# Where the weight steps of a two-layer Fourier and MLP kernel stand among its matrix products: fixed places in inner products instead of every second place

## Chip, cores and metric

One core of a Trainium2 chip runs the kernel alone. The metric is the device time in microseconds of one execution; 2741.95 us is the median of three runs (2740.89 to 2742.17). The engines are TensorE (PE, matrix products; PEld is its weight load), VectorE (DVE), ScalarE (ACT), GpSimd (POOL) and SyncE (SP), which here only issues DMAs. Each engine works through its own instructions in program order and waits for the others by semaphores.

## Reference

Two layers, each a Fourier mixing block and an MLP on 2048 tokens of width 576, with an inner width of 4608, in float32:

```python
def _A_ref(x, dft_seq_re, dft_seq_im, dft_hid_re, dft_hid_im):
    a = jnp.einsum("bsd,ed->bse", x, dft_hid_re)
    b = jnp.einsum("bsd,ed->bse", x, dft_hid_im)
    return jnp.einsum("ts,bse->bte", dft_seq_re, a) - jnp.einsum("ts,bse->bte", dft_seq_im, b)

def _B_ref(x, w1, b1, w2, b2):
    y = _layernorm(x, axis=-1)
    h = _gelu(jnp.einsum("bsd,df->bsf", y, w1) + b1)
    return jnp.einsum("bsf,fd->bsd", h, w2) + b2

x = x + _A_ref(_layernorm(x), ...)
x = x + _B_ref(_layernorm(x), ...)
x = x + _A_ref(_layernorm(x), ...)
x = x + _B_ref(_layernorm(x), ...)
```

Both layers use the same weights and the same Fourier matrices.

## The kernel before

**Arithmetic.** Every float32 factor is split into a high part in the type float32r and the low rest: ACT writes the high part (`hi`, `high`), VectorE subtracts it from the source (`lo`, `low`). A product is then three matmuls (high by high, high by low, low by high). On top of that, products of two-by-two blocks are done as seven block products instead of eight, numbered 1 to 7 and done in the order 1, 6, 2, 5, 7, 3, 4 (`ORDER`); the sums of blocks that this needs are made on VectorE and POOL ahead of it, and the products are put together while they are taken out of PSUM.

**Stages.** A layer runs the sequence transform (`Sequence`: the normalized input times the Fourier matrix along tokens; sixteen token tiles, the first two in plain products, fourteen by seven products each, `run`, L687 on), then for each half of the tokens the hidden transform (`hidden`, matrices from `dh`) and the MLP (`mlp`). All matmuls but the transposes are recorded at one line, L206, all adds at L196 and all subtracts at L199, since helpers issue them.

**The MLP of a half.** 18 inner products (`inner`, first weights w1, bias and gelu) and 9 times seven outer products (`outer`, second weights w2, two half-products each). A group is: an even inner product (7 block products of 7 matmuls of 512 columns), the four outer products of the first list in `OUTER` for the group before (1, 6, 5, 3: 8 half-products of 12 matmuls of 288 columns), an odd inner product, and the three outer products of the second list (7, 4, 2: 6 half-products); 49 + 96 + 49 + 72 = 266 matmuls. Behind each block product or half-product `advance()` is called. It counts the place within the group in `at[0]`: 0 to 6 are the even inner product, 7 to 14 the four outer products, 15 to 21 the odd inner product, 22 to 27 the three outer products; `at[1]` counts on without a reset. After `advance` of an outer half-product VectorE adds the bank to the sum in SBUF (L196, 128x576), which frees the bank; there are two pairs of banks for each side, so a bank is written again two half-products later, and the next inner product uses the same banks. In the slots of outer products and in the block products of the next inner one, `work` takes one of eight `step(n)`s that split gelu's results into parts.

**First weights' steps.** `weights()` (L272 on) is a generator that makes the 126 parts of the first weights (18 times seven) in layer 0: `load` brings four raw blocks of an inner product (`in_w`, four times 192 KB), `high(n)` and `low(n)` split part n (ACT L272, L273; VectorE L199, 128x384), POOL makes the next sum of blocks, and `keep(n)` stores the part to `w_parts` from ACT's queue and loads raw blocks for the next inner product on SP's queue. It yields after each `low(n)` with `high(n+1)`, and after each `keep(n)`: two pumps for a part. `pump()` takes it one yield on. In the sequence transform of layer 0 `pump()` is called twice behind each product but the third (product 2); in the MLP `advance` calls it; `load_w`, which loads parts for coming inner products from SP's queue, calls it as often as the part asked for is not yet made. Both halves and layer 1 read the parts back.

**Second weights' parts.** In the MLP of the first half of layer 0 the second weights are split too: `make(g)` gives fourteen steps for group g, a `hi` (ACT L1080) and a `lo` (VectorE L199, 128x576, and in most a subtract on POOL) for each of the seven parts, with the places at which `advance` takes them; parts needed by the first outer products are made one group ahead. `soon` puts stores and raw loads two places later.

**Queues.** SP issues nearly all loads and stores of activations, in program order, and a DMA that has to wait (for its target to be read out) holds up all behind it. `b1t` holds the first biases; it is loaded behind the sequence transform of layer 0.

Of the kernel before, what the change touches and what calls it, by code (L numbers as in the profile page):

```python
# [20 lines left out]
NG = NQ // 2  # L21
# [36 lines left out]
EXTRA_AT = 7424  # L58
EARLY_X = (12800, 9344, 8192)
EARLY_T = 10496  # L60
H_AT = (8704, 22400)
C2_AT = (OWN_AT, 37760)
Y_AT = (RN - Y_N, 0)
# [92 lines left out]
def spectral_mixer(ctx: ExitStack, tc: tile.TileContext, x, dh, c0, cs, w1, b1, w2, b2, out):  # L156
# [29 lines left out]
    b1t = const.tile([P, 2 * NQ], F32, name="b1t")  # L186
    middle = const.tile([P, 1], F32, name="middle")

    def dma(dst, src):
        nc.sync.dma_start(dst, src)  # L190
# [61 lines left out]
    def weights():  # L252
        b = raw(4, 3 * P)
        a22, a21, a11, a12 = (b[:, k] for k in range(4))
        g = nc.gpsimd
        steps = ((4, a22, lambda: add(g, a22, a21, a22)), (1, a11, lambda: sub(g, a21, a11, a21)),
                 (5, a22, lambda: sub(g, a11, a22, a11)), (2, a12, lambda: sub(g, a12, a12, a11)),
                 (7, a21, None), (6, a11, None), (3, a12, None))

        def load(q, k):  # L260
            if q < NQ:
                dma(b[:, k], w1[q][:, k])

        def at(n):
            return stage(3, 5 * P)[:, n % 3]

        def cut(a):
            return a.rearrange("p (k f) -> p k f", f=P)

        def high(n):  # L270
            src, t = cut(steps[n % 7][1]), cut(at(n))
            nc.scalar.activation(t[:, 1:4:2], src[:, 0:3:2], AF.Copy)  # L272
            nc.scalar.activation(t[:, 2], src[:, 1], AF.Identity, bias=power[:, 2:3], scale=middle)  # L273

        def low(n):

            q, k = divmod(n, 7)
            i, src, then = steps[k]
            t = cut(at(n))
            sub(nc.vector, t[:, 0:5:2], cut(src), t[:, 1:4].bitcast(F32))  # L280
            if then:
                then()

        def keep(n):

            q, k = divmod(n, 7)
            put(w1s[q, steps[k][0] - 1], at(n).bitcast(F32))
            if k in (2, 4, 5, 6):
                load(q + 1, (2, 4, 5, 6).index(k))
            if k == 6:  # L290
                made[0] = q + 1

        for k in range(4):
            load(0, k)
        yield
        high(0)
        for n in range(7 * NQ):
            yield
            low(n)
            if n + 1 < 7 * NQ:  # L300
                high(n + 1)
            yield
            keep(n)
        stage.free()
        raw.free()
# [11 lines left out]
    class Sequence:  # L317
# [362 lines left out]
        def run(self, hidden):  # L680
            for p in range(NP):
                while self.ready <= p:
                    next(self.pieces)
                self.first_mms(p)

            for _ in self.pieces:
                pass  # L687
            hidden.reserve()
            if not self.early:

                for k in range(KH):
                    dma(dhd[k], dh[k])
            steps = self.steps
            self.low(*steps[1])
            self.high(*steps[2])
            for t in range(PLAIN):
                self.first_post(t)
            for n, (t, i) in enumerate(steps):
                self.load_c()
                if n + 2 < len(steps):  # L700
                    self.low(*steps[n + 2])
                if i == 2 and t + 1 < NT:
                    self.sums(t + 1)
                self.load_c()
                if n + 3 < len(steps):
                    self.high(*steps[n + 3])
                self.mms(t, i)
                self.post(t, i)
                if t == NT - 1:
                    hidden.begin(self, ORDER.index(i))  # L710
                if i != 2:
                    pump()
                    pump()
            for k in range(2):
                self.L[k].free()
            self.own.close()
            for z in self.Z:
                z.free()
            hidden.take()
# [314 lines left out]
    def mlp(hid, store, first, before, after):  # L1034
# [39 lines left out]
        def make(g):  # L1074
            b11, b12, b22, b21, x = (rv[:, k] for k in range(5))
            pool = nc.gpsimd

            def hi(i, src):
                got2[g, i] = c2.take()
                nc.scalar.activation(got2[g, i](2, 2, DH)[:, :, 0], src, AF.Copy)  # L1080

            def lo(i, src):
                t = got2[g, i](2, 2, DH)
                sub(nc.vector, t[:, :, 1], src, t[:, :, 0].bitcast(F32))
                b = got2[g, i]
                soon(lambda: put(w2s[g, i - 1], b(2, 2 * DH).bitcast(F32)))

            def soon(step):
                kept.append((at[1] + 2, step))

            one = [lambda: hi(1, b11), lambda: (lo(1, b11), sub(pool, b11, b12, b11), sub(pool, x, b22, b11))]
            six = [lambda: hi(6, x), lambda: (lo(6, x), sub(pool, x, b21, x))]
            five = [lambda: hi(5, b11), lambda: (lo(5, b11), soon(lambda: load_raw(g + 1, 0)))]
            three = [lambda: hi(3, b22), lambda: (lo(3, b22), sub(pool, b12, b22, b12), soon(lambda: load_raw(g + 1, 2)))]
            seven = [lambda: hi(7, b12), lambda: (lo(7, b12), soon(lambda: load_raw(g + 1, 1)))]
            four = [lambda: hi(4, x), lambda: lo(4, x)]
            two = [lambda: hi(2, b21), lambda: (lo(2, b21), soon(lambda: load_raw(g + 1, 3)))]
            late = (5, 6, 7, 8, 9, 10, 11, 12, 13, 14) if g == NG - 1 else (0, 1, 9, 10, 15, 16, 17, 18, 19, 20)
            return list(zip((24, 25, 26, 27), one + five)), list(zip(late, six + three + seven + four + two))

        at = [0, 0]

        def advance(to=None):
            at[1] += to is None
            if to is None and at[1] % 2:
                pump()
            while kept and kept[0][0] <= at[1]:
                kept.pop(0)[1]()
            while due and due[0][0] <= (at[0] if to is None else to):
                due.pop(0)[1]()  # L1110
            at[0] += 1
# [163 lines left out]
        for g in range(NG + 1):  # L1275
            at[0] = 0
            if first and g:
                if g == 1:
                    soon, late = make(0)
                    due.extend((n, step) for n, (_, step) in enumerate(soon))  # L1280
                    late[:2] = [(n + 4, step) for n, step in late[:2]]
                due.extend(late)
                if g < NG:
                    soon, late = make(g)
                    due.extend(soon)
# [38 lines left out]
    for layer in range(2):  # L1324
        src, to = (xd, out) if layer else (x, xd)
        hid = Hidden(0, src, layer == 1)
        seq.run(hid)
        if layer == 0:
            dma(b1t, b1)
        for half in range(2):  # L1330
            here = hid

# [58 lines left out]
```

## Time and profile before

| what | us |
|---|---|
| median of the runs | 2741.95 |
| the profiled execution's own time | 2745.19 |
| its span | 2743.0 |
| of it sequence transform, layer 0, about | 0 to 390 |
| hidden transform and MLP, first half of layer 0, about | 390 to 911 |
| the same, second half | 911 to 1405 |
| layer 1 | 1405 to 2743 |

The stretches are read from the chain of waits (transposes of the hidden transform begin at 390.25 and at 921.79, and the load of the intermediate result for layer 1 at 1410.04). The granted TensorE clock over the span is 0.997. The page gives busy time of each engine; a group of instructions is a line, an engine, an operation, what it writes and reads, and a count, with busy time, mean duration and, behind the second bar, idle time before them and what ended it. In a timeline a row has the start, the time, the engine and line, and in brackets the idle time before it with what ended it. A busy PE is not PE at its peak: the matmuls' ends are modelled.

### The profile page before, as it was taken

To read this page: it belongs to the slowest core of one execution; us is meant where nothing else is said; L and a number is where in the kernel's file an instruction comes from. 1 tells how busy PE (TensorE), PEld (TensorE's weight loads), DVE (VectorE), ACT (ScalarE), POOL (GpSimd) and SP (SyncE) were. 2 spreads that over 40 slices of the span, in tenths; PEclk is the share of its full clock that TensorE was granted. 3 is DMA by queue.
4 is the path that set the end of the run, shared out by engine and by line. 5 is a ranking of instruction groups with operands and counts; after the bars stand their busy time and mean duration, and the time that the engine had idled before them with its cause. 6 is when DMAs were issued, how large, how long until landed. Compare 5 with 4: busy or idle time off the path is not lost.

```text
span 2743.0 us, 45225 instructions
## 1 busy us (share of the span) xinstructions
PE 2670.2 (97%) x17488; PEld 2500.8 (91%) x17488; DVE 1772.7 (65%) x2582; ACT 1103.2 (40%) x1838; POOL 796.7 (29%) x746
## 2 busy tenths in 40 slices
PE   8999999999899999999999999999999999999999
PEld 7999999888788989998899999998989899898988
DVE  8788866777666465556577666565555556655555
ACT  6555544544443243333344333344333324433331
POOL 5132224543533432222241000042222224222222
PEclk9999999999999999999999999999999999999999
DMA  5677774877757646667563333537666673666664
GB/s 200 227 247 242 241 263 161 283 257 275 259 191 251 240 136 193 191 195 227 166 223 120 119 121 124 201 102 208 193 195 193 195 257 130 196 194 195 193 195 153
DMA packets 209285, 544.90 MB, mean 199 GB/s; under 512 B 22048, under 2 KB 56864, under 8 KB 208928
## 3 DMA queue, kind: packets, MB, share of 16 engines
q1 hardware_dynamic: 181856, 463.56, 53.5%
q10 hardware_dynamic: 27216, 78.46, 7.3%
q8 instruction: 138, 2.26, 0.3%
q14 instruction: 75, 0.61, 0.1%
HBM read 429.87 MB, written 114.72 MB: 199 GB/s over the span
## 4 chain that ended last, share of the span: by engine, by line
PE 84%; DVE 7%; issue 3%; DMA 2%; ACT 2%; POOL 2%; SPq 0%; ACTq 0%; DVEq 0%; POOLq 0%
PE bank L206 83%; DVE R L199 3%; DVE A L196 1%; DVE A L199 1%; PE bank L837 1%; POOL A L199 1%; DMA A<-in_cs 0%; DMA A<-in_c 0%; ACT A L246 0%; DMA R<-w_parts 0%; POOL R L199 0%; ACT R L632 0%; DVE bank L196 0%; PE bank L908 0%; DVE moments L221 0%
## 5 line engine op out<-in xcount | busy, mean ns | idle before, releaser
L206 PE MATMUL bank<-R 128*128 128x288 f32 (+2 forms) x16972 | 2621.3, 315 | 60.5 <-DVE A L196 27.9
L206 PEld LDWEIGHTS bank<-R 128*128 128x128 f32 x16972 | 2446.3, 189 | 227.4 <-DVE A L196 44.5
L196 DVE TENSOR_TENSOR A<-bank,A 128x576 f32<-128x576 f32 (+3 forms) x808 | 567.4, 710 | 549.1 <-PE bank L206 466.7
L199 POOL TENSOR_TENSOR R<-A,R 128x512 fp32r<-128x512 f32 x288 | 378.9, 1326 | 933.3 <-ACT R L1203 888.0
L199 DVE TENSOR_TENSOR R<-A,R 128x1024 fp32r<-128x1024 f32 (+10 forms) x521 | 492.3, 968 | 61.5 <-ACT R L632 23.2
L196 POOL TENSOR_TENSOR A<-A 128x576 f32<-128x576 f32 (+2 forms) x102 | 136.2, 1340 | 583.6 <-ACT A L670 376.4
L1142 ACT ACTIVATE bank<-bank,b1t 128x512 f32<-128x512 f32 (+1 forms) x224 | 144.8, 646 | 392.4 <-DVE bank L196 267.0
L1203 ACT ACTIVATE R<-A 128x512 fp32r<-128x512 f32 x288 | 175.8, 628 | 254.3 <-DVE A L199 95.9
L632 ACT ACTIVATE R<-A 128x1024 fp32r<-128x1024 f32 x196 | 205.4, 1056 | 173.6 <-DVE A L199 104.2
L199 POOL TENSOR_TENSOR A<-A 128x384 f32<-128x384 f32 (+2 forms) x154 | 197.1, 1281 | 235.1 <-DVE R L199 132.0
L196 DVE TENSOR_TENSOR bank<-bank,A 128x512 f32<-128x512 f32 (+1 forms) x228 | 152.5, 671 | 164.8 <-PE bank L206 164.4
L199 DVE TENSOR_TENSOR R<-bank,R 128x512 fp32r<-128x512 f32 x336 | 209.8, 639 | 56.2 <-ACT R L202 50.4
L199 DVE TENSOR_TENSOR A<-A 128x1024 f32<-128x1024 f32 (+3 forms) x132 | 141.5, 1077 | 6.1 <-ACT A L246 2.1
L1203 ACT ACTIVATE R<-bank 128x512 fp32r<-128x512 f32 x216 | 122.0, 594 | 37.3 <-PE bank L206 34.7
L1169 ACT ACTIVATE A<-bank 128x512 f32<-128x512 f32 (+1 forms) x76 | 43.8, 576 | 225.5 <-PE bank L206 223.0
L199 DVE TENSOR_TENSOR A<-bank,A 128x512 f32<-128x512 f32 x144 | 97.9, 680 | 0.0
L202 ACT ACTIVATE R<-bank 128x512 fp32r<-128x512 f32 (+1 forms) x112 | 50.0, 492 | 86.6 <-PE bank L837 79.2
L246 ACT ACTIVATE A<-A,moments 128x576 f32<-128x576 f32 x64 | 53.7, 862 | 56.9 <-POOL moments L229 31.6
L1142 ACT ACTIVATE A<-bank,b1t 128x512 f32<-128x512 f32 (+1 forms) x76 | 50.7, 667 | 57.7 <-DVE bank L196 57.7
L672 DVE SCALAR_TENSOR_TENSOR A<-A 128x288 f32<-128x288 f32 x28 | 16.0, 571 | 86.8 <-POOL A L196 86.8
L273 ACT ACTIVATE R<-A,power,middle 128x128 fp32r<-128x128 f32 x126 | 60.8, 482 | 0.0
L1080 ACT ACTIVATE R<-A 128x576 fp32r<-128x576 f32 x63 | 42.3, 679 | 40.6 <-POOL A L199 36.4
(58 smaller groups left out, 620.2 us busy)
## 6 DMA issues: line engine op xcount, KB each, us to landing
R<-w_parts SPq DMA_DIRECT2D x504, 320.0 KB, 3.5
R<-w_parts SPq DMA_DIRECT2D x189, 576.0 KB, 3.7
A<-in_cs SPq DMA_DIRECT2D x112, 512.0 KB, 4.3
w_parts<-R ACTq DMA_DIRECT2D x126, 320.0 KB, 4.2
w_parts<-R ACTq DMA_DIRECT2D x63, 576.0 KB, 5.8
uv_mid<-A SPq DMA_DIRECT2D x32, 576.0 KB, 3.1
A<-in_w SPq DMA_DIRECT2D x72, 192.0 KB, 4.3
R<-dh_parts SPq DMA_DIRECT2D x23, 576.0 KB, 10.4
```

Of the source, the lines that this page charges most:

```text
L196: engine.tensor_tensor(dst, a, b, op=op)
L199: engine.tensor_tensor(dst, a, b, op=OP.subtract)
L202: nc.scalar.activation(hi, src, AF.Copy)
L206: nc.tensor.matmul(o, a, b, start=start, stop=stop, skip_group_check=True)
L246: nc.scalar.activation(dst, src, AF.Identity, bias=mv[:, 4:5], scale=mv[:, 3:4])
L273: nc.scalar.activation(t[:, 2], src[:, 1], AF.Identity, bias=power[:, 2:3], scale=middle)
L632: nc.scalar.activation(self.cells[t, i](2, NP, P)[:, 0], self.source(t, i), AF.Copy)
L837: nc.tensor.transpose(at, v[:, k], ident)
L1080: nc.scalar.activation(got2[g, i](2, 2, DH)[:, :, 0], src, AF.Copy)
L1142: nc.scalar.activation(dst, src, AF.Gelu_apprx_tanh, bias=bias(f))
L1169: nc.scalar.activation(up, o, AF.Copy)
L1203: nc.scalar.activation(H[q, k](2, TC)[:, 0], src, AF.Copy)
```

## The change

```diff
 EARLY_T = 10496
+BEHIND = (3, 4, 5, 6, *range(14, 22))
...
         for k in range(4):
             load(0, k)
-        yield
+        for _ in range(4):
+            yield
         high(0)
...
             if not self.early:
-
+                dma(b1t, b1)
                 for k in range(KH):
                     dma(dhd[k], dh[k])
...
-            late = (5, 6, 7, 8, 9, 10, 11, 12, 13, 14) if g == NG - 1 else (0, 1, 9, 10, 15, 16, 17, 18, 19, 20)
-            return list(zip((24, 25, 26, 27), one + five)), list(zip(late, six + three + seven + four + two))
+            if g == NG - 1:
+                return (list(zip((24, 25, 26, 27), one + five)),
+                        list(zip(range(5, 15), six + three + seven + four + two)))
+            return (list(zip((24, 25), one)),
+                    list(zip((0, 1, 2, 3, 9, 10, 15, 16, 17, 18, 19, 20), five + six + three + seven + four + two)))
...
             at[1] += to is None
-            if to is None and at[1] % 2:
+            if to is None and at[0] in BEHIND:
                 pump()
...
-                    late[:2] = [(n + 4, step) for n, step in late[:2]]
+                    late[:4] = [(n + 2, step) for n, step in late[:4]]
...
         seq.run(hid)
-        if layer == 0:
-            dma(b1t, b1)
         for half in range(2):
```

In the MLP a pump is taken at twelve fixed places of a group (3 to 6, and 14 to 21), six parts, instead of at every second place (fourteen pumps, seven parts). Part 5 of the second weights is made at places 0 and 1 of the group that uses it instead of 26 and 27 of the group before, and part 6 moves from 0 and 1 to 2 and 3; part 1 stays at 24 and 25. In the sequence transform the generator yields three times more before its first split, and the biases are loaded ahead of the nine copies of `dh`. With the change 81 parts are made when the MLP begins, before it 83; the last one is stored in the inner product 16 (counted from 0), before in 13.

The lines of the changed kernel are one to three higher. Three places of the new order:

VectorE in the MLP of the first half, the three outer products at the end of a group (places 24 to 27): `A<-bank,A 128x576` is the add that frees a bank, `R<-bank,R` and `A<-bank,A 128x512` are splits and sums of gelu's results, `128x3x128` is `low` of a first-weights step and `128x2x288` is `lo` of a second-weights part. Before:

```order
L199 TENSOR_TENSOR R<-bank,R 128x512
L199 TENSOR_TENSOR A<-bank,A 128x512
L199 TENSOR_TENSOR R<-A,R 128x2x288
L196 TENSOR_TENSOR A<-bank,A 128x576
L199 TENSOR_TENSOR R<-bank,R 128x512
L199 TENSOR_TENSOR A<-A,bank 128x512
L199 TENSOR_TENSOR R<-A,R 128x3x128
L196 TENSOR_TENSOR A<-bank,A 128x576
L199 TENSOR_TENSOR R<-A,R 128x2x288
L196 TENSOR_TENSOR A<-bank,A 128x576
```

and with the change:

```order
L200 TENSOR_TENSOR R<-bank,R 128x512
L200 TENSOR_TENSOR A<-bank,A 128x512
L200 TENSOR_TENSOR R<-A,R 128x2x288
L197 TENSOR_TENSOR A<-bank,A 128x576
L200 TENSOR_TENSOR R<-bank,R 128x512
L200 TENSOR_TENSOR A<-A,bank 128x512
L197 TENSOR_TENSOR A<-bank,A 128x576 x2
L200 TENSOR_TENSOR A<-bank,A 128x512
```

The step of the first weights ahead of the add of place 26 and part 5's subtract ahead of the add of place 27 are gone from there.

ACT at the start of the products of the sequence transform of layer 0: L632 splits a block for a coming product, L662 to L670 take products out of PSUM, L272 and L273 are `high` of a first-weights step. Before:

```order
L632 ACTIVATE R<-A 128x1024
L662 ACTIVATE A<-bank 128x288
L272 ACTIVATE R<-A 128x2x128
L273 ACTIVATE R<-A,power,middle 128x128
L632 ACTIVATE R<-A 128x1024
L272 ACTIVATE R<-A 128x2x128
L273 ACTIVATE R<-A,power,middle 128x128
L193 DMA w_parts<-R 128x640
L632 ACTIVATE R<-A 128x1024
L666 ACTIVATE A<-bank 128x288
```

and with the change:

```order
L634 ACTIVATE R<-A 128x1024
L664 ACTIVATE A<-bank 128x288
L634 ACTIVATE R<-A 128x1024 x2
L668 ACTIVATE A<-bank 128x288
L634 ACTIVATE R<-A 128x1024
L670 ACTIVATE A<-bank 128x288
L273 ACTIVATE R<-A 128x2x128
L274 ACTIVATE R<-A,power,middle 128x128
L273 ACTIVATE R<-A 128x2x128
L274 ACTIVATE R<-A,power,middle 128x128
```

The first split of a weight block moved from behind the first product to behind the fourth.

SP at the end of the sequence transform of layer 0: `in_w` are raw first weights, `uv_mid` results of the transform, `in_x` the residual rows of the hidden transform. Before:

```order
L190 DMA A<-uv_mid 128x1152 x2
L190 DMA R<-dh_mid 128x576 x6
L190 DMA A<-in_w 128x384
L190 DMA R<-dh_mid 128x576 x3
L190 DMA A<-uv_mid 128x1152
L190 DMA A<-in_w 128x384
L190 DMA uv_mid<-A 128x1152
L190 DMA A<-in_w 128x384
L190 DMA b1t<-in_b 128x36
L190 DMA A<-in_x 128x2x288 x2
```

and with the change:

```order
L191 DMA A<-in_w 128x384
L191 DMA R<-dh_mid 128x576 x2
L191 DMA A<-in_w 128x384
L191 DMA R<-dh_mid 128x576 x7
L191 DMA A<-uv_mid 128x1152
L191 DMA A<-in_w 128x384
L191 DMA uv_mid<-A 128x1152
L191 DMA A<-in_x 128x2x288 x2
```

The raw load and the biases between `uv_mid` and `in_x` are gone from there, and a raw load stands ahead of seven instead of three loads of `dh_mid`.

## The prediction

> **What bounds the kernel now.** I read the page first: the busy line, then the chain of work that ended last.
>
> ```profile
> PE 2670.2 (97%) x17488; PEld 2500.8 (91%) x17488; DVE 1772.7 (65%) x2582; ACT 1103.2 (40%) x1838; POOL 796.7 (29%) x746
> PE bank L206 83%; DVE R L199 3%; DVE A L196 1%; DVE A L199 1%; PE bank L837 1%; POOL A L199 1%; DMA A<-in_cs 0%; DMA A<-in_c 0%; ACT A L246 0%; DMA R<-w_parts 0%; POOL R L199 0%; ACT R L632 0%; DVE bank L196 0%; PE bank L908 0%; DVE moments L221 0%
> ```
>
> TensorE sets the time, and the change takes no matmul away. All it can win or lose are the places where the chain leaves PE for another engine. The change touches layer 0 alone: the weight steps run in its sequence transform and in the MLP of its first half. So the next view is busy time by stretch, one stretch for each group of that MLP (two inner products, seven outer ones, 266 matmuls), with one group of layer 0's second half, which does the same matmuls with no weight steps, as the last row.
>
> ```profile
> core 0: us, PE busy (x) PEld busy (x) DVE busy (x) ACT busy (x) POOL busy (x), PEclk, DMA share, GB/s
> 563.71:613.31 49.60, 46.35 (x267) 41.07 (x267) 36.24 (x53) 23.37 (x47) 21.53 (x16) 1.00 0.73 263
> 662.91:712.47 49.56, 46.27 (x267) 41.02 (x267) 36.24 (x53) 23.35 (x47) 21.54 (x16) 1.00 0.73 263
> 712.47:765.83 53.36, 48.03 (x267) 42.20 (x267) 36.26 (x53) 23.34 (x46) 21.48 (x16) 0.97 0.64 233
> 765.83:812.30 46.47, 46.15 (x266) 40.96 (x267) 31.58 (x47) 18.53 (x32) 16.79 (x12) 1.00 0.64 220
> 1072.01:1117.26 45.25, 45.22 (x267) 40.85 (x267) 25.50 (x38) 14.59 (x24) 10.26 (x8) 1.00 0.65 194
> ```
>
> The reader is to see three periods for the same matmuls: 49.6 us with both kinds of weight steps, 46.47 us once the first weights are finished (they run out in the group that ends at 765.83; the second weights' steps go on), and 45.25 us with neither. So the first weights' steps cost a group 49.60 - 46.47 = 3.13 us although VectorE is idle for a quarter of it. PE's timeline tells where.
>
> ```profile
> 590.05 19.84 PE L206 MATMUL bank<-R 128*128 128x512 f32 x109 [1.54 <-DVE A L196]
> 611.36 26.76 PE L206 MATMUL bank<-R 128*128 128x288 f32 x157 [1.47 <-DVE A L196]
> 750.77 11.63 PE L206 MATMUL bank<-R 128*128 128x512 f32 x67 [2.07 <-DMA R<-w_parts]
> 788.74 46.23 PE L206 MATMUL bank<-R 128*128 128x288 f32 x266 [0.21 <-DVE A L196]
> ```
>
> Two long waits a group, both for VectorE's add out of PSUM (L196): one at the end of the three outer products, before the next inner product may write the bank, one inside the four outer products. The first group without them waits 0.21 us once.
>
> **The groups.** An outer half-product is 12 matmuls (some 1.6 us), and its bank is wanted again two half-products later, so VectorE may be about one slot late. What makes it later:
>
> ```profile
> 579.09 0.55 DVE L199 TENSOR_TENSOR R<-A,R 128x384 fp32r<-128x384 f32 x1
> ...
> 587.09 0.68 DVE L199 TENSOR_TENSOR A<-A,bank 128x512 f32<-128x512 f32 x1
> 587.69 1.64 DVE L199 TENSOR_TENSOR R<-A,R 128x384 fp32r<-128x384 f32 x1
> 589.25 0.74 DVE L196 TENSOR_TENSOR A<-bank,A 128x576 f32<-128x576 f32 x1
> ...
> 608.32 2.31 DVE L199 TENSOR_TENSOR R<-A,R 128x384 fp32r<-128x384 f32 x2
> 610.55 0.74 DVE L196 TENSOR_TENSOR A<-bank,A 128x576 f32<-128x576 f32 x1
> ```
>
> The 128x384 subtract is `low()` of a first-weights step. Alone it takes 0.55 us (at 579.09, in an inner product); at 587.69 it takes 1.64 us, and the add that PE waits for stands right behind it. At 608.32 the same subtract and one of a second-weights part take 2.31 us ahead of the next such add. POOL was at work over the first of them:
>
> ```profile
> 585.99 4.19 POOL L199 TENSOR_TENSOR A<-A 128x576 f32<-128x576 f32 x3 [8.56 <-DVE R L199]
> ```
>
> In the changed order no `low()` of the first weights stands between these adds: at places 7 to 13 and 22 to 27 no step is pumped, and place 14 always gets a `keep` (12 pumps a group, an even number, so the phase holds), which is a store on ACT's queue and nothing on VectorE. The subtract of part 5 at place 27 goes too. What is left in the outer products is part 1 at places 24 and 25 and part 3 at 9 and 10. That is less than the group 765.83:812.30 carried, which still had part 5 at 26 and 27; there the place of the 1.64 us was empty:
>
> ```profile
> 789.20 0.68 DVE L199 TENSOR_TENSOR A<-A,bank 128x512 f32<-128x512 f32 x1
> 789.80 0.75 DVE L196 TENSOR_TENSOR A<-bank,A 128x576 f32<-128x576 f32 x1
> ```
>
> So I price a changed group at 46.47 us. From 514.12 to 765.83, less the 3.8 us by which the last group there is over its equals, there is room for 247.9 / 49.6 = five groups with the pair of waits: 5 x 3.13 = **15.7 us**. Part 5 itself I price at nothing: its `lo` stood behind the add of place 26, not ahead of it, and its `hi` only held ACT. Bounds: 45.25 us a group for all nine would give 5 x 4.35 + 3 x 1.2 = 25 us; nothing gained if the waits only move.
>
> Where the steps go: six of them a group, to places 3 to 6 and 15 to 21. A slot there is 7 matmuls of 512, about 1.63 us, with one PSUM add of 0.70 us. In the odd inner product VectorE now has four 128x384 subtracts (places 15, 17, 19, 21) between three 128x576 ones (16, 18, 20), so one a slot:
>
> ```profile
> L199 DVE TENSOR_TENSOR R<-A,R 128x576 fp32r<-128x576 f32 x35 | 33.0, 943 | 0.0
> L199 DVE TENSOR_TENSOR R<-A,R 128x384 fp32r<-128x384 f32 x35 | 27.7, 793 | 0.0
> ```
>
> By their means over the waiting groups that is 0.70 + 0.94 or 0.70 + 0.79 us in 1.63 us: full at the worst, and hidden, since PE wants a bank again only one or two slots later. If the cover fails, the price is that of the one inner product that is crowded before (the third, which starts the second weights):
>
> ```profile
> 498.73 1.90 PE L206 MATMUL bank<-R 128*128 128x512 f32 x7 [0.36 <-DVE A L196]
> 501.61 5.74 PE L206 MATMUL bank<-R 128*128 128x512 f32 x36 [0.98 <-DVE bank L196]
> 507.79 8.45 PE L206 MATMUL bank<-R 128*128 128x288 f32 x57 [0.44 <-POOL R L199]
> ```
>
> That is 1.8 us. This product gets its steps at places 3 and 5 now instead of 2 and 6; I put **1 us of loss** there, bounds 0 and 1.8. On SP's queue a raw load (`in_w`) waits for VectorE and POOL, and loads of parts stand behind it. The two that are wanted within the same inner product are issued at its first two places; the pumps at 3 to 6 and, but for place 14's, from 16 on put the raw loads behind these. Steps end later (in the seventeenth inner product instead of the fourteenth), and one is forced there; its part is read 13 places after its store, so I cost it at nothing.
>
> The Trainium skill, SBUF — State Buffer, section Who interferes with whom, says that a VectorE instruction with two SBUF inputs and a GpSimd one that reads SBUF lock each other out for a whole instruction. The 0.55 and 1.64 us above agree with that. By that rule the change only moves the loss, since POOL's work stays in the inner products; that is the first rival below.
>
> **The start of the sequence transform.** The first pump issued the raw loads and the second, in the same product, put `high(0)` on ACT behind them.
>
> ```profile
> 67.64 13.01 PE L206 MATMUL bank<-R 128*128 128x288 f32 x96 [1.46 <-ACT A L586]
> 83.03 0.53 PE L206 MATMUL bank<-R 128*128 128x288 f32 x2 [2.38 <-ACT R L632]
> 84.84 14.48 PE L206 MATMUL bank<-R 128*128 128x288 f32 x96 [1.28 <-DVE R L199]
> ...
> 81.23 0.42 ACT L272 ACTIVATE R<-A 128x256 fp32r<-128x256 f32 x1 [7.25 <-DMA A<-in_w]
> ...
> 83.03:90.00 6.97, 5.69 (x29) 5.45 (x30) 6.94 (x6) 3.92 (x8) 2.55 (x2) 0.76 0.34 122
> ...
> 1474.00 4.24 PE L206 MATMUL bank<-R 128*128 128x288 f32 x30 [0.67 <-DVE R L199]
> ```
>
> ACT stood 7.25 us for the load, and the split of the fifth block (L632), queued behind it, was late: PE lost 2.38 + 1.28 us, and, with a granted clock of 0.76 after that, 96 matmuls took 14.48 instead of 13.01 us, 1.47 more: 5.1 us. With three more empty yields `high(0)` stands behind the fourth product, when the load is about in. What is late next is shown by layer 1, which has no weight steps: its sixth product waits 0.67 us for VectorE. So 5.1 - 0.7 = **4.4 us**; bounds 0 (the wait comes back a few products later, since VectorE is busy 6.94 of the 6.97 us after it) and 5.1.
>
> **The hand-over to the hidden transform.** SP's queue and what waited for it:
>
> ```profile
> 389.23 0.38 SPq L190 DMA_DIRECT2D uv_mid<-A  x1
> 392.66 0.33 SPq L190 DMA_DIRECT2D A<-in_w  x1
> 393.04 0.67 SPq L190 DMA_DIRECT2D b1t<-in_b  x1
> 393.76 1.31 SPq L190 DMA_DIRECT2D A<-in_x  x2
> ...
> 399.03 0.76 DVE L196 TENSOR_TENSOR A<-bank,A 128x576 f32<-128x576 f32 x1 [3.92 <-DMA A<-in_x]
> ...
> 399.84 0.40 PE L837 MATMUL bank<-ident,A 128*128 128x128 f32 x1 [3.58 <-DVE A L196]
> ...
> 400.24 8.65 PE bank L206 x54
> 409.88 7.19 PE bank L206 x54
> ```
>
> The residual rows (`in_x`) stood behind a raw load that waited until 392.66 and behind the biases (0.67 us). Both are gone from that place in the new order of SP: the biases go ahead of the sequence steps, and with 1.5 steps fewer done, no raw load falls between `uv_mid` and `in_x`. So `in_x` can issue some 4 us sooner, as much as VectorE waited (3.92 us). PE wins 3.58 us and the slow clock after it, 8.65 - 7.19 = 1.46: **5.0 us**; bounds 0.7 (the biases alone) and 5.0. The other raw load now stands ahead of seven loads of `dh_mid`, which have a product's time in hand.
>
> **The sum.** 15.7 + 4.4 + 5.0 - 1.0 = 24.1 us. The profiled execution took 2745.19 us with a span of 2743.0, 3.2 us over the median of 2741.95. Its group 712.47:765.83 is 3.8 us longer than its equals, with one load of parts (2.07 us of wait, clock 0.97); I take that for a mishap of this execution and count no gain on it. From the median: 2741.95 - 24.1 = **2718 us**.
>
> **Rivals.** *The waits move into the inner products.* For it: POOL goes on working there, and beside POOL a subtract took 1.64 - 0.55 = 1.09 us longer. Against it: a bank has a slot in hand there. Three subtracts a group are moved; if half of them met POOL with nothing in hand, 5 x 3 x 1.09 / 2 = 8 us would be lost: 2726 us. The rule of the skill above is this rival's. *Only the groups gain*: the two early waits come back behind the next late load; 2718 + 9.4 = 2727 us. *Slower*: if every inner product from the fourth to the eighteenth became as crowded as the third, 15 x 1.8 = 27 us against 25 gained, and with the clock's fall after them more: 2745 to 2755 us. It decides from 1.7 us lost in each inner product; it needs VectorE over a slot late in every one, which the means do not give. *The change does not do what it says*, the steps being forced in the outer products after all, when parts are wanted: the waits would stay, 2742 us; but only one pump is forced, in an inner product.
>
> **How the numbers follow.** Forecast (2711 to 2722): 0.62. Waits moved into the inner products: 0.13. Only the groups: 0.11. More than forecast, if also the rests of 1.2 us a group go with part 5 (below 2711): 0.06. The change does not do what it says, and the time stays within 0.2% (5.5 us, about what can be told from no change): 0.03. Slower: 0.05. The range, 2710 to 2729, leaves some 0.2 out. Faster: 0.92.
>
> **What would show it.** Right: groups of 46 to 46.5 us from 514 on, no wait over 0.5 us before places 12 and 0; 128x384 subtracts near 0.6 to 0.9 us; ACT's 7.25 us gone; no PE wait over 1 us at the hand-over. Wrong: PE waits for L196 with 512-wide matmuls after them in mid inner product, or the early waits some products later.

## The result and the profile after

The changed kernel takes 2727.76 us (median of five runs, 2727.39 to 2728.42) against 2740.89 us of the kernel before beside it (five runs, 2738.03 to 2742.17). The ratio is 0.9955, with a 95% interval of 0.994 to 0.9969: 13.1 us are gained, where 24.1 were forecast. The profiled execution has a span of 2726.0 us. Busy time by engine on its page:

```profile
PE 2665.1 (98%) x17488; PEld 2499.7 (92%) x17488; DVE 1764.2 (65%) x2582; ACT 1101.0 (40%) x1838; POOL 797.4 (29%) x746
```

It is the same work; what changed is where TensorE waits.

TensorE's timeline of the changed kernel, at the start of the sequence transform, answers to the rows at 67.64, 83.03 and 84.84 of the prediction:

```profile
68.00 26.24 PE L207 MATMUL bank<-R 128*128 128x288 f32 x194 [1.47 <-ACT A L588]
94.85 30.41 PE L207 MATMUL bank<-R 128*128 128x288 f32 x228 [0.61 <-DVE R L200]
```

The waits of 2.38 and 1.28 us are gone and one of 0.61 us has come, some products later. The chain of waits at the hand-over, with its start and duration in the first two columns, has no other engine in it any more:

```profile
385.14 0.98 PE bank L839 x9
...
391.29 7.19 PE bank L207 x54
...
399.46 7.20 PE bank L207 x54
```

In TensorE's timeline the same transposes are this row:

```profile
384.97 1.15 PE L839 MATMUL bank<-ident,A 128*128 128x128 f32 x9
```

There they began at 390.25 before, so they begin 5.3 us sooner. In the chain the block of 54 matmuls that began at 409.88 begins at 399.46, 10.4 us sooner. Up to here the times are those that the prediction gave. The groups, by the view of busy time by stretch:

```profile
553.23:602.01 48.78, 46.36 (x267) 41.06 (x267) 34.00 (x52) 22.26 (x44) 20.09 (x15) 1.00 0.74 257
602.01:651.25 49.24, 46.01 (x266) 41.02 (x267) 34.42 (x52) 22.22 (x44) 20.98 (x16) 1.00 0.72 254
651.25:697.67 46.42, 46.13 (x266) 41.05 (x267) 34.38 (x52) 22.64 (x44) 20.85 (x16) 1.00 0.77 269
697.67:744.88 47.21, 46.02 (x267) 41.01 (x267) 33.89 (x52) 22.22 (x44) 21.48 (x16) 1.00 0.76 270
744.88:794.19 49.31, 46.26 (x266) 41.06 (x267) 34.96 (x52) 22.54 (x44) 20.25 (x15) 1.00 0.73 253
```

One group of the five took the 46.47 us forecast for all. TensorE's timeline shows what the others wait for:

```profile
497.02 0.91 PE L207 MATMUL bank<-R 128*128 128x288 f32 x5 [0.98 <-DVE A L197]
499.57 26.71 PE L207 MATMUL bank<-R 128*128 128x288 f32 x152 [1.64 <-POOL R L200]
...
575.04 46.50 PE L207 MATMUL bank<-R 128*128 128x288 f32 x266 [2.28 <-DVE A L197]
624.04 21.42 PE L207 MATMUL bank<-R 128*128 128x288 f32 x121 [2.50 <-DVE A L197]
...
767.34 49.54 PE L207 MATMUL bank<-R 128*128 128x288 f32 x290 [2.95 <-DVE A L197]
...
840.04 24.47 PE L207 MATMUL bank<-R 128*128 128x288 f32 x145 [0.96 <-DVE A L197]
```

The old pair of waits (1.5 us each, before places 12 and 0) is gone. New ones of 2.3 to 3.0 us stand in the three outer products, three half-products after an odd inner product. The name VectorE there is only the last link. VectorE and ACT before the first of them:

```profile
566.99 0.80 DVE L200 TENSOR_TENSOR R<-A,R 128x576 fp32r<-128x576 f32 x1
...
568.61 0.55 DVE L200 TENSOR_TENSOR R<-A,R 128x384 fp32r<-128x384 f32 x1
569.61 0.76 DVE L197 TENSOR_TENSOR A<-bank,A 128x576 f32<-128x576 f32 x1 [0.45 <-PE bank L207]
573.04 0.69 DVE L200 TENSOR_TENSOR R<-bank,R 128x512 fp32r<-128x512 f32 x1 [2.68 <-ACT R L1208]
```

```profile
568.96 1.56 ACTq L194 DMA_DIRECT2D w_parts<-R  x2
570.57 0.69 ACT L1147 ACTIVATE A<-bank,b1t 128x512 f32<-128x512 f32 x1 [4.40 <-DVE A L197]
```

VectorE's subtracts there take 0.55 to 0.80 us, and then it stands idle for 2.68 us, for a split by ACT. ACT in its turn stands idle for 4.40 us ahead of a gelu (L1147), and a store of a part is what stands at the head of its queue. The chain of waits says what the store waited for:

```profile
562.03 6.84 DMA A<-in_w
...
568.89 0.04 ACTq L194
...
570.57 0.69 ACT A L1147
...
573.65 1.35 DVE A L197 x2
...
575.04 1.99 PE bank L207 x13
```

A store to `w_parts` waits for the landing of a raw load, with which it shares no data. (Ahead of the waits at 624.04 and 767.34 the chain has the same links, behind loads of parts that took 7.18 and 7.63 us.) The program's order shows why: in it each of the 1370 DMAs, from SP's queue or ACT's, counts its end on one of eight counters that are taken in turn, and waits for the DMA that had this counter before. Rows of ACT in the program:

```
L194 DMA w_parts<-R 128x640 [waits DMAHW6_49,DVE_49]
L194 DMA w_parts<-R 128x640 [waits DMAHW1_49,DVE_49]
```

So a store may go out only when the DMA eight places before it has landed, and in none of the traces, of this kernel or another here, does a DMA go out sooner. The raw load issued at 562.03 has the same counter as the store issued at 568.96. On SP's queue such a wait holds other DMAs; on ACT's queue it holds gelu and the splits.

How much that is can be read from each trace. Call a store held if it goes out on ACT's queue within 0.15 us of the landing of the DMA eight places before it. In the groups 23 stores are held so after the change and 5 before it, and ACT stands idle ahead of them for 20.4 us after and 3.2 us before. The DMA views of one group each (columns: what, queue, count, size, median us from issue to landing), before from 563 to 613 us and after from 552 to 602:

```profile
w_parts<-R ACTq DMA_DIRECT2D x7, 320.0 KB, 4.3
...
A<-in_w SPq DMA_DIRECT2D x4, 192.0 KB, 3.6
```

```profile
w_parts<-R ACTq DMA_DIRECT2D x7, 320.0 KB, 5.0
...
A<-in_w SPq DMA_DIRECT2D x4, 192.0 KB, 5.6
```

The fixed places put a load or a store of the first weights behind nearly every block product of the odd inner product. In this group the loads of 192 KB take 2.0 us longer to land and the stores 0.7; over all the waiting groups (before from 514 to 714, after from 504 to 745) the medians are 3.4 and 4.8 us for the loads and 4.2 and 4.7 us for the stores.

### The profile page after: what moved, and what is told of

The parts are those of the page before. It is cut to its first block, busy times and chain, and to the rows that moved or that the text cites. A ratio compares the mean times of both kernels' runs of the same rounds, so it can differ in the third digit from the quotient of the medians.

```text
span 2726.0 us, 45200 instructions
## 1 busy us (share of the span) xinstructions
PE 2665.1 (98%) x17488; PEld 2499.7 (92%) x17488; DVE 1764.2 (65%) x2582; ACT 1101.0 (40%) x1838; POOL 797.4 (29%) x746
## 4 chain that ended last, share of the span: by engine, by line
PE 73%; DVE 5%; DMA 3%; issue 2%; ACT 2%; POOL 1%; ACTq 0%; SPq 0%; DVEq 0%; POOLq 0%
PE bank L207 71%; DVE R L200 2%; DMA A<-in_w 2%; DVE A L197 1%; PE bank L839 1%; DVE A L200 1%; DMA R<-w_parts 1%; POOL A L200 1%; ACT R L1208 0%; DVE moments L237 0%; POOL R L200 0%; PE bank L910 0%; ACT bank L1147 0%; ACT A L247 0%; DVE moments L222 0%
## 5 line engine op out<-in xcount | busy, mean ns | idle before, releaser
L200 DVE TENSOR_TENSOR R<-A,R 128x1024 fp32r<-128x1024 f32 (+8 forms) x521 | 485.2, 953 | 59.1 <-ACT R L634 27.5
L1147 ACT ACTIVATE bank<-bank,b1t 128x512 f32<-128x512 f32 (+1 forms) x224 | 144.6, 646 | 363.1 <-DVE bank L197 241.7
L1147 ACT ACTIVATE A<-bank,b1t 128x512 f32<-128x512 f32 (+1 forms) x76 | 50.6, 666 | 79.4 <-DVE bank L197 56.3
L273 ACT ACTIVATE R<-A 128x256 fp32r<-128x256 f32 x126 | 51.7, 410 | 41.1 <-DMA A<-in_w 20.9
```

The source lines that it names most:

```text
L200: engine.tensor_tensor(dst, a, b, op=OP.subtract)
L1147: nc.scalar.activation(dst, src, AF.Gelu_apprx_tanh, bias=bias(f))
```

## The experiments

Twelve kernels ran, each beside the kernel before, in three batches on one chip each (medians of before 2739.49, 2739.28 and 2739.5 us). "Groups" is read from each run's one trace: from the wait for POOL that ends the third inner product (499.57 after) to the wait of 0.94 to 1.03 us just behind the last of the first weights' steps (840.04 after). "ACT idle" is ACT's idle time in that stretch ahead of held stores, as above; it is 3.2 us before and 20.4 us in the changed kernel. The prediction's 15.7 us would have brought this stretch from 346.5 us (350.34 in the profile before, less the 3.8 us of its mishap) to 330.8; the changed kernel has 340.5.

| kernel | median us | ratio, 95% interval | groups, us | ACT idle, us |
|---|---|---|---|---|
| early_only | 2721.34 | 0.9929, 0.9916 to 0.9941 | 335.9 | 3.2 |
| mlp_only | 2739.0 | 0.9998, 0.9989 to 1.0007 | 348.0 | 21.0 |
| puts_sp | 2721.04 | 0.9927, 0.9914 to 0.9939 | 333.3 | 5.1 |
| extra_dma | 2733.98 | 0.9977, 0.9967 to 0.9988 | 348.6 | 30.6 |
| phase_back | 2729.41 | 0.9964, 0.995 to 0.9977 | 341.4 | 4.4 |
| every_second | 2718.37 | 0.9923, 0.9909 to 0.9936 | 334.7 | 3.2 |
| five_back | 2727.54 | 0.9955, 0.9942 to 0.9967 | 338.2 | 14.4 |
| spread | 2727.7 | 0.9959, 0.9946 to 0.9971 | 340.2 | 18.7 |
| before_sp | 2738.19 | 0.9994, 0.9985 to 1.0003 | 346.4 | 0.0 |
| mlp_sp | 2725.14 | 0.9937, 0.9924 to 0.9951 | 332.5 | 3.0 |
| every_second_sp | 2717.74 | 0.9917, 0.9903 to 0.993 | 332.1 | 0.1 |
| every_second_sp2 | 2716.17 | 0.9911, 0.9898 to 0.9925 | 332.4 | 0 |

(In mlp_only and mlp_sp the third inner product does not end in that wait; there the stretch is counted back by 1893 matmuls, as many as it has in the others.)

**early_only.** The early parts of the change alone; the MLP is that of the kernel before.

```diff
-        yield
+        for _ in range(4):
+            yield
...
+                dma(b1t, b1)
                 for k in range(KH):
...
-        if layer == 0:
-            dma(b1t, b1)
```

> Only the three empty yields and the earlier load of the biases, with every second place pumped as before. Theory (the early waits are worth what the two traces show, 10.4 us by the third block of the hidden transform, and stand apart from the groups): 10 us under the kernel before. Rival (a gain at the start is given back in the MLP, whose loads fall otherwise): 5 us or less under it.

It gained 18.2 us, more than the whole change; neither expectation had that. The yields do something else besides: they are three, an odd number, so that `low` and `keep` have changed places in the MLP. TensorE's timeline:

```profile
546.14 27.90 PE L206 MATMUL bank<-R 128*128 128x288 f32 x169 [0.50 <-DVE A L196]
574.25 18.23 PE L206 MATMUL bank<-R 128*128 128x288 f32 x97 [0.21 <-DVE A L196]
592.97 24.73 PE L206 MATMUL bank<-R 128*128 128x288 f32 x145 [0.50 <-DVE A L196]
```

The pair of 1.5 us has become 0.50 and 0.2 us. This group takes 592.97 - 546.14 = 46.83 us, with no fixed place and seven parts a group; the next three take 47.6, 48.2 and 46.8 us, the two longer ones with a third wait, of 0.44 and 0.91 us.

**mlp_only.** The other half of the change: the fixed places and the second weights' places.

```diff
-        for _ in range(4):
-            yield
+        yield
...
-                dma(b1t, b1)
...
+        if layer == 0:
+            dma(b1t, b1)
```

> Only the fixed places and the moved second weights' parts; one empty yield and the biases' load as before. Theory (the five pairs of waits are gone, but waits behind ACT's stores have come in the same groups): 2 to 4 us under the kernel before, groups of 46.4 to 49.3 us. Rival (the places gain what was predicted, and the early parts lose it): 14 us under it.

It gained 0.5 us, which cannot be told from nothing and is less than either expected. The fixed places by themselves move the waits, and those that come are longer:

```profile
532.45 46.25 PE L207 MATMUL bank<-R 128*128 128x288 f32 x266 [1.55 <-DVE A L197]
...
631.42 22.65 PE L207 MATMUL bank<-R 128*128 128x288 f32 x121 [3.02 <-DVE A L197]
```

**puts_sp.** The changed kernel, with the MLP's stores of first-weights parts on SP's queue instead of ACT's. What is stored, and when it is ready, stays.

```diff
-            put(w1s[q, steps[k][0] - 1], at(n).bitcast(F32))
+            (put if n < 81 else dma)(w1s[q, steps[k][0] - 1], at(n).bitcast(F32))
```

> The changed kernel, with the stores of first-weights parts in the MLP issued from SP's queue instead of ACT's; nothing else moves. Theory (ACT stands at a store of a part until an earlier DMA of either queue has landed, and the gelu behind it is late): the 2.3 to 3.0 us waits in the three outer products go, groups of 46.4 us, 6 to 10 us under the changed kernel, unless SP's loads of parts then come late, which would show as PE waits for them. Rival (VectorE is held by POOL in the inner products): groups stay at 47 to 49 us, within 2 us of the changed kernel.

It gained 6.7 us over the changed kernel, as the theory had it; the two intervals, 0.9914 to 0.9939 and 0.994 to 0.9969, do not overlap. Two waits over 1 us are left in the groups, and the chain puts a DMA and ACT's queue ahead of both. The later one:

```profile
750.84 6.95 DMA R<-w_parts
...
757.81 0.02 ACTq L194
...
760.28 0.80 PE bank L207 x4
```

That is a store of a second-weights part, which this kernel leaves on ACT's queue.

**extra_dma.** The changed kernel, with one small DMA more on SP's queue behind each store of a first-weights part in the MLP, 45 in all; it copies 16 rows of the biases to a spare place and nobody reads it.

```diff
+    spared = nc.dram_tensor("spare", (45, 16, 2 * NQ), F32, kind="Internal").ap()
...
+            if n >= 81:
+                dma(spared[n - 81], b1[0:16])
```

> The changed kernel with one more DMA of 2.3 KB, from DRAM to DRAM on SP's queue, behind each store of a part in the MLP (45 in all, 0.1 MB). Theory A (what holds the stores is the count of DMAs under way, eight for both queues): waits grow, 4 to 15 us over the changed kernel. Theory B (it is the bytes, which make each landing late): within 1.5 us of the changed kernel.

It lost 6.2 us by the medians (the intervals overlap by 0.0002) and 8.1 in the groups (340.5 to 348.6), though a copy has 2.3 KB. So bytes can't be the cause. The count of transfers can, if only eight may be under way: 34 stores are held now, where 23 were, and ACT's idle time ahead of them goes from 20.4 to 30.6 us. What the copies cost beside that, as issue time on SP's queue, was not told apart.

**phase_back.** early_only with four added yields, an even number.

```diff
-        yield
+        for _ in range(5):
+            yield
...
```

> As early_only (the kernel before with the biases sent in the sequence transform and more empty yields ahead of the first step), but with four added yields in place of three, so that a lo of the first weights falls on the same places of the MLP as in the kernel before (2, 6, 10, 14 and so on) and not on those between them. Phase theory (early_only gained some 10 us at the start and some 8 us because its subtracts fell at other places): the start keeps its gain, the groups are back at 49.6 us with waits of 1.5 us for VectorE before places 12 and 0, and the time is 2728 to 2731 us. Rival (the groups gain because the steps come later or because the hand-over is clean, whatever their phase): 2720 to 2723 us.

The time came as the phase theory had it, the groups only by half: they take 48.5 to 49.3 us and not 49.6. The wait before place 12 or 0 came back once a group, the other stayed small:

```profile
530.96 19.81 PE L206 MATMUL bank<-R 128*128 128x512 f32 x109 [1.57 <-DVE A L196]
...
579.42 19.87 PE L206 MATMUL bank<-R 128*128 128x512 f32 x109 [1.56 <-DVE A L196]
599.64 26.70 PE L206 MATMUL bank<-R 128*128 128x288 f32 x157 [0.35 <-DVE A L196]
```

VectorE and, behind it, POOL ahead of the small wait at 599.64:

```profile
597.70 1.22 DVE L199 TENSOR_TENSOR R<-A,R 128x384 fp32r<-128x384 f32 x2
598.83 0.75 DVE L196 TENSOR_TENSOR A<-bank,A 128x576 f32<-128x576 f32 x1
```

```profile
598.48 2.71 POOL L199 TENSOR_TENSOR A<-A 128x384 f32<-128x384 f32 x2 [7.89 <-DVE R L199]
```

And POOL in the kernel before, at the place of the 2.31 us:

```profile
608.51 1.51 POOL L199 TENSOR_TENSOR R<-A,R 128x512 fp32r<-128x512 f32 x1 [6.88 <-ACT R L1203]
```

The two subtracts that took 2.31 us before (the row at 608.32 in the prediction) took 1.22 us, in the same order and at the same place. Before, POOL began 0.2 us after the first of them and worked over most of the two; here it begins 0.8 us after, when the second was under way. (With four yields another of the seven parts falls on the place, with other sums for POOL; that this is why POOL comes later is argued, not shown.) The rule of the Trainium skill that the prediction named (SBUF — State Buffer, Who interferes with whom) fits both rows. So of early_only's 10.5 us in the groups (346.4, as before_sp has them without the mishap, to 335.9) 5.0 are there at the old phase too, and 5.5 go with the phase, the kind of step that falls on a place. By the medians the phase is worth 8.1 us (2729.41 to 2721.34).

**every_second.** The changed kernel with pumps at every second place again: early_only and the second weights' new places.

```diff
-            if to is None and at[0] in BEHIND:
+            if to is None and at[1] % 2:
```

> The changed kernel, but the steps of the first weights at every second place, as in the kernel before, in place of the fixed places; the early parts and the second weights' part moved out of places 26 and 27 stay. It is early_only with that one part of the second weights moved. Theory (moving that part is worth nothing, and the fixed places lose 6.5 us against the phase that the added yields give): within 1.5 us of early_only's 2721.3 us. Rival (moving it is worth 2 us or more, either way): below 2719.5 or above 2723.5 us.

It gained 20.9 us, 2.8 more than early_only, so by the medians the rival; but the intervals of the two overlap widely and the groups differ by 1.2 us only. Whether the new places of parts 5 and 6 are worth anything stays open here.

**five_back.** The changed kernel with parts 5 and 6 at their old places.

```diff
-            return (list(zip((24, 25), one)),
-                    list(zip((0, 1, 2, 3, 9, 10, 15, 16, 17, 18, 19, 20), five + six + three + seven + four + two)))
+            return (list(zip((24, 25, 26, 27), one + five)),
+                    list(zip((0, 1, 9, 10, 15, 16, 17, 18, 19, 20), six + three + seven + four + two)))
...
```

> The changed kernel with the second weights' fifth part back at places 26 and 27 of the outer products and the sixth at 0 and 1, as in the kernel before; all else stays. Theory (that part's place is worth nothing, its subtract stands behind the add that TensorE waits for): 2726 to 2729.5 us, as the changed kernel. Rival (its four places in the inner product crowd the third one and the rest): 2723 to 2725 us; the other rival (back in the outer products it delays the next group's first inner product): 2730 us and more.

The same as the changed kernel (0.9955 both): as the prediction priced it, that move is worth nothing that can be told there. In the two traces it takes 2.3 us from the groups and has them begin 1.2 us later (500.80 for 499.57).

**spread.** The changed kernel with the twelve places further apart and two stores a group in outer products.

```diff
-BEHIND = (3, 4, 5, 6, *range(14, 22))
+BEHIND = (2, 3, 4, 5, 6, 8, 15, 17, 18, 20, 21, 23)
...
-        for _ in range(4):
+        for _ in range(5):
```

> The changed kernel with the twelve places of a group spread: loads and subtracts stay in the inner products (2, 4, 6, 15, 18, 21) but for one raw load, and two of the six stores a group go to the first places of the outer products (8 and 23); one more empty yield puts the kinds of step on these places. Theory (the loss is ACT held at stores bunched into the odd inner product, behind loads issued just before them): ACT's waits of 4 to 6 us at a store go, groups take 46.4 to 47.2 us, the time is 2716 to 2722 us. Rival (the subtracts in the inner products are the trouble, VectorE being late there): groups stay near 48.5 us, 2726 us and more.

The theory's numbers missed: no gain over the changed kernel. Its profile is of the slowest of its five runs (2733.57 us), with a wait of 2.00 us for ACT at the end of the sequence transform (0.89 us in phase_back, which has as many yields; none in the changed kernel). But the groups are as long as the changed kernel's too (340.2 us). The chain ahead of its largest wait is the one above again:

```profile
732.02 6.93 DMA R<-w_parts
...
738.97 0.02 ACTq L194
...
743.06 14.59 PE bank L207 x81
```

So the store still stood behind a transfer that took 7 us, and moving two of six did not free ACT: 24 stores are held, with 18.7 us of idle time ahead of them. The rival has the time, but not the cause, since what is late is ACT. The theory names the queue that is late, but spreading the places did not cure it, so that the bunching holds the stores is not shown by this run.

**before_sp** and **mlp_sp.** The edit of puts_sp (with 83 for 81, the parts made when their MLP begins) in the kernel before and in mlp_only.

> The kernel before, with the stores of first-weights parts in the MLP issued from SP's queue in place of ACT's. Theory (a store holds ACT only where it is put among many transfers, at the fixed places of the changed kernel; in the kernel before the waits come from VectorE's subtracts): the pair of 1.5 us waits a group stays, within 2 us of the 2740 us before. Rival (stores on ACT's queue cost the kernel before as much as the changed one): 5 us or more faster, 2735 us and less.

> mlp_only (the fixed places and the second weights' places alone, with the start and the hand-over of the kernel before), with the stores of first-weights parts in the MLP issued from SP's queue. Theory (the stores on ACT's queue take from the groups what the fixed places give them): 5 to 9 us under mlp_only's 2739 us, so 2730 to 2734 us, with groups of 46.5 to 47 us. Rival (the gain from SP's queue in the changed kernel came of its other places): 2737 us and more.

Before, the stores on ACT's queue cost nothing that can be told (1.3 us; the interval of the ratio holds 1), and the pair of 1.5 us stays. With the fixed places they cost 13.9 us (2739.0 to 2725.14), more than the 5 to 9 expected. TensorE's timeline of mlp_sp, from the first full group on:

```profile
577.64 46.28 PE L207 MATMUL bank<-R 128*128 128x288 f32 x266 [1.20 <-DVE A L197]
624.77 49.43 PE L207 MATMUL bank<-R 128*128 128x288 f32 x290 [0.85 <-DVE A L197]
674.40 92.86 PE L207 MATMUL bank<-R 128*128 128x288 f32 x532 [0.20 <-DVE A L197]
767.47 46.24 PE L207 MATMUL bank<-R 128*128 128x288 f32 x266 [0.21 <-DVE A L197]
```

Two groups from 674.40 on take 93.07 us, 46.5 each: the price that the prediction gave a changed group. The whole stretch has 332.5 us, where that price for every group would have brought 330.8. Against before the MLP's part of the change now gains 14.4 us, where the prediction had 15.7 less 1.0.

**every_second_sp** and **every_second_sp2.** The best places with the stores of the first weights, and then of the second weights too, on SP's queue.

```diff
-                soon(lambda: put(w2s[g, i - 1], b(2, 2 * DH).bitcast(F32)))
+                soon(lambda: dma(w2s[g, i - 1], b(2, 2 * DH).bitcast(F32)))
```

> every_second (first-weights steps at every second place behind the added yields, second weights as in the changed kernel), with the stores of first-weights parts in the MLP issued from SP's queue: a try at the best version. Theory (at every second place the store is seldom held, and what is left, 0.5 and 0.2 us a group, is VectorE's): 2715 to 2718.5 us, no more than 3 us under every_second's 2718.4. Rival (ACT's stores still cost some 1 us a group there): 2713 us and less; the other rival (a store on SP's queue holds the loads behind it): 2720 us and more.

> every_second_sp with the stores of the second weights' parts on SP's queue too, so that ACT issues no store in the MLP. Theory: ACT's waits for transfers are all gone, little is left to win: within 1.5 us of every_second_sp. Rival (a store on SP's queue stands ahead of the loads of parts): 2 us slower or more, with waits of TensorE for loads of parts.

The first came as the theory had it, the second just outside (1.6 us less, in a stretch other than the groups, and with intervals that overlap). 2716.17 us, ratio 0.9911 with 0.9898 to 0.9925, is the fastest of all; its groups keep one wait of 0.50 us for VectorE.

## Why the prediction was partly right

**The time and its sign** held: 2727.76 us lies in the range, at its upper end, 9.8 us above the 2718 us of the sum and above the 2711 to 2722 held likeliest. Two of the four terms were twice too large or more, so that the time still lies in the range is in part owed to the range's width.

**The start of the sequence transform** was right: 4.4 us forecast, and by the transposes behind it 5.3 came. The next late thing is a wait for VectorE of 0.61 us (forecast 0.7).

**The hand-over** was right in its cause, and its size came by luck: 10.4 - 5.3 = 5.1 us between the two profiles, forecast 5.0. Some 3 us of that belong to the one profile of before from which the term was read. before_sp has the same hand-over; TensorE waits 2.33 us there and not 3.58, and the 54 matmuls behind it take 7.20 us and not 8.65, at a granted clock of 1.00 from 400 to 410 and not 0.83:

```profile
398.40 0.33 PE L837 MATMUL bank<-ident,A 128*128 128x128 f32 x1 [2.33 <-DVE A L196]
```

```profile
398.72 7.20 PE bank L206 x54
```

mlp_only has it so too (1.99 and 7.19 us). Against these two the change wins some 2 to 2.5 us at the hand-over, half of the 5.0.

**The third inner product** lost 2.2 us (the lead of 10.4 us is 8.2 at 499.57) and not 1.0; the bound was 1.8. Its waits (0.98 and 1.64 us among them) are the rows at 497.02 and 499.57 above. The prediction feared VectorE there; the chain ahead of the longer wait begins with a raw load and goes through POOL. puts_sp loses nearly as much there (1.9 us), so ACT's first-weights stores are not the cause:

```profile
489.13 5.17 DMA A<-in_w
```

**The mishap** of 3.8 us was rightly left out: before_sp, which has the same places, doesn't have it (its groups take 346.4 us, the kernel before without the mishap 346.5). By the profiles the lead behind the groups is 858.13 - 840.04 = 18.1 us, less the mishap 14.3, and less the 3 us of the hand-over 11.3; by the medians the gain is 13.1. TensorE's row in the profile before from which that is:

```profile
858.13 12.21 PE L206 MATMUL bank<-R 128*128 128x288 f32 x67 [0.94 <-DVE A L196]
```

**The groups** were the step that failed: "So I price a changed group at 46.47 us" and from it 15.7 us, where the stretch gained 6.0 (346.5 to 340.5). What the step says of VectorE is right in the main: the waits behind the 1.64 us and 2.31 us subtracts are gone. Some subtracts of the first weights are still slow (8 of the 40 in the stretch take over 1 us, up to 1.65; before, 11 of 37), but puts_sp has the same 8 slow ones and few waits. What it says of ACT is wrong: a `keep` was counted as "a store on ACT's queue and nothing on VectorE" and so as nothing. A store waits there for the DMA eight before it, and with the fixed places this one has often not landed (23 held stores in place of 5): ACT 4.40 us idle, then VectorE, then TensorE. That it has not landed because loads and stores stand so close together in the odd inner product is argued, not shown. puts_sp and mlp_sp show the price by taking the stores off that queue alone: 6.7 us of the changed kernel, 13.9 of mlp_only, and nothing that can be told of the kernel before. With the stores away mlp_sp comes within 1.7 us of the prediction's own groups (332.5 and 330.8). The prediction looked for such a wait on SP's queue only.

**What was not seen** is that the early edit changes the MLP as well. The three yields shift which step falls on which place, and at every second place the early edit is worth 10.5 us of groups (early_only), 5.5 of them by that shift. The fixed places set these places anew, and most of what they gain is lost to ACT: 6.0 us are left.

**The rivals.** "The waits move into the inner products" gave 2726 us and "only the groups gain" 2727 us, both near the time, both for reasons that the runs refute: the subtracts are not what is late (puts_sp leaves them as they are and wins 6.7 us), and it is the early gains that stayed while most of the groups' did not. The slower case needed 1.7 us in each inner product and got it in none but the third.

What stays open: why the stores cost 13.9 us in mlp_only and 6.7 in the changed kernel though ACT's idle time ahead of held stores is the same (21.0 and 20.4 us; between the two lies the phase of the fixed places, which was not varied alone with the stores on SP's queue), and why spread's stores are held nearly as long as the changed kernel's.

## What to carry to other kernels

In this kernel stores on a computing engine's queue cost nothing that could be told as long as they could mostly go out at once (1.3 us before), and 6.7 or 13.9 us where they could not. Ahead of moving a DMA, read what it waits for, its place among the last transfers included, and what is queued behind it on the issuing engine. Where stores are held, try the queue of an engine that computes nothing. Read a term that rests on one wait in one execution in a second execution too. Where steps alternate on fixed places, an edit that adds one step far ahead shifts all that follow: compare versions at the same phase, and try both.

## What was not expected of the hardware

45 copies of 2.3 KB, for which nobody waits, cost 6.2 us (extra_dma). In one group the loads of 192 KB took a median of 5.6 us to land after the change and 3.6 us before it (4.8 and 3.4 us over all the waiting groups), at about the same traffic (12.82 MB in 50 us after, 13.16 MB before). And two VectorE subtracts at the same place take 1.22 us where POOL begins 0.8 us after the first of them and 2.31 us where it begins 0.2 us after (597.70 in phase_back, 608.32 before).
